# A static instruction order planned for two DMA queues that together get 0.76 of the full rate, with two more chunks of keys transposed on TensorE and half the margin on transposing DMAs

## The chip, the cores and the metric

The kernel runs on one core of a Trainium2 chip. The metric is the device time of one execution in microseconds (us). A run that takes over 1.5% more than the fastest run of the same kernel in the same call (one batch of runs on one chip) is called slow; all others are fast. A ratio is the mean time of one kernel's fast runs over the mean of the other's fast runs of the same rounds, so it is not quite the ratio of the medians quoted. "Span" is the time from the first to the last instruction of the one execution that was profiled, about 2 us less than its device time.

## The reference, cut to what matters

Causal linear attention with a decay per head (4 batches, 8 heads, 768 positions, head size 64), done in blocks with a state that is carried on, and after it a feed-forward layer with SiLU over the 3072 x 512 result.

```python
for b in range(nb):                       # blocks of one sequence
    intra = einsum('bhic,bhjc->bhij', qb, kb) * Dmask
    intra = einsum('bhij,bhjd->bhid', intra, vb)
    inter = einsum('bhid,bhde->bhie', qb * lam_pow, kv_state)
    out[:, :, sl] = intra + inter
    kv_state = lam_block * kv_state + einsum('bhsd,bhse->bhde', kb * rev_pow, vb)
...
x = out as (3072, 512)
h = x @ w_in                              # 512 x 2048
return (h / (1 + exp(-h))) @ w_out        # 2048 x 512
```

## The kernel before

The work is cut into 24 chunks of 128 positions and 12 FFN groups of two chunks. Chunks 0 to 5 (batch 0) use one form of attention. Chunks 6 to 23 use another and are loaded in nine segments of two chunks each: a q load, eight pieces of k, eight pieces of v. The first segment is issued on the SP queue, the other eight on GpSimd's.

Every instruction is first described as an operation with its dependences. A small planner, run at build time, then simulates engines and DMA queues and writes each engine's instructions down in the order in which its simulation started them. On the chip each engine follows that order whether or not the simulation was right: an instruction that waits holds up all that stand behind it on the same engine. These are the planner's parts that the change touches.

```python
LATE = 60000.0      # ns of the plan's own time
LADD = 6000.0
EFF = 0.9
STEP = 12.5
...
        live = [f for f in queue if queue[f]]          # "HW" (SP) and "POOL" (GpSimd)
        for f in live:
            cap = STEP * (0.5 * EFF if len(live) == 2 else 1.0)
            ...                                        # serves the queue's first transfer
                op.seen = t + 700.0 + (1.5 * op.bytes / op.rate if op.rate == 170.0 else 0.0)
...
                    margin = LADD if e == "PE" and t > LATE else 0.0
                    for d in op.deps:
                        s = d.seen + (margin if d.bytes else 0.0)   # d.bytes: d is a DMA
```

`seen` is when the plan believes that a transfer is visible. TensorE reads no load directly; the only DMAs it depends on directly are transposing ones, so the margin concerns these alone. Whether a chunk's keys are transposed on TensorE (with an eviction, a copy out of TensorE's output memory PSUM, by VectorE or ScalarE) or by a DMA is a matter of its number.

```python
    def prep_k(c):
        if c < NPET:                                   # NPET = 10
            ...
                for s in range(2):
                    for p in range(NP):                # NP = 4
                        nc.tensor.transpose(ps.tile[:, s, p, :], cols(s, p), ident)
            ...                                        # eviction on VectorE or ScalarE
        else:
            ...
                nc.sync.dma_start_transpose(out=tk.tile..., in_=kb.tile...)
```

## Time and profile before

| | before |
|---|---|
| device time, median of the first 3 runs | 229.15 us (228.57 to 237.23) |
| span of the profiled run | 228.1 us (device time 230.11 us, mean clock 0.987) |
| TensorE busy | 213.9 us (94%) |
| TensorE waits after the first 30 us | five, 7.1 us together |
| VectorE + ScalarE idle at the head of a cast or scaling of a load, until a DMA landed | 65 us |

No fast run of this kernel was profiled. So wherever its trace is set beside that of a fast run below, a slow run stands beside a fast one, and the difference is likely larger than between fast runs; the ratios are of fast runs alone.

The last row is the sum, in the list of who waited for whom, of the waits of VectorE and ScalarE on DMA at the lines that turn loaded q, k and v into bf16 or scale them (k and v of batch 0, 2.4 us, left out). These are VectorE's two largest (columns: us in total, times, longest):

```profile
DVE vs L574 <- DMA big<-in_v_dram: 17.9, 6, 6.4
DVE kseg L422 <- DMA big<-in_k_dram: 10.9, 5, 5.8
```

The lines that show TensorE's own waits are in the prediction.

### The profile page before, as it was taken

To read this page: it belongs to the slowest core of one execution; us is meant where nothing else is said; L and a number is where in the kernel's file an instruction comes from. 1 tells how busy PE (TensorE), PEld (TensorE's weight loads), DVE (VectorE), ACT (ScalarE), POOL (GpSimd) and SP (SyncE) were. 2 spreads that over 40 slices of the span, in tenths; PEclk is the share of its full clock that TensorE was granted. 3 is DMA by queue.
4 is the path that set the end of the run, shared out by engine and by line. 5 is a ranking of instruction groups with operands and counts; after the bars stand their busy time and mean duration, and the time that the engine had idled before them with its cause. 6 is when DMAs were issued, how large, how long until landed. Compare 5 with 4: busy or idle time off the path is not lost.

```text
span 228.1 us, 5382 instructions
## 1 busy us (share of the span) xinstructions
PE 213.9 (94%) x2177; PEld 150.5 (66%) x2177; DVE 121.0 (53%) x260; ACT 116.5 (51%) x218; POOL 88.9 (39%) x152
## 2 busy tenths in 40 slices
PE   8998999999999999999996987997799999999991
PEld 5686876665975875966853864783584885865840
DVE  3887864766897836557408624832626554202011
ACT  5669797763775682844821641642461361441510
POOL 3000000198979568596953964946300000000000
PEclk9999999999999999999997999999999999999997
DMA  5999999999966999999999999999790301202204
GB/s 140 333 295 388 328 331 333 278 237 223 237 150 129 226 204 170 233 152 231 178 171 155 198 177 138 171 211 137 147 182 19 78 3 33 62 0 46 49 0 92
DMA packets 49400, 39.15 MB, mean 172 GB/s; under 512 B 28896, under 2 KB 39136, under 8 KB 49376
## 3 DMA queue, kind: packets, MB, share of 16 engines
q1 hardware_dynamic: 43984, 26.22, 56.3%
q0 software_dynamic: 5248, 12.59, 26.7%
q8 instruction: 17, 0.28, 0.6%
q14 instruction: 7, 0.06, 0.1%
q10 hardware_dynamic: 144, 0.00, 0.0%
HBM read 27.27 MB, written 6.29 MB: 147 GB/s over the span
## 4 chain that ended last, share of the span: by engine, by line
DMA 37%; PE 29%; POOL 17%; SPq 6%; issue 4%; ACT 3%; DVE 1%; POOLq 0%
DMA big<-in_k_dram 23%; POOL big L406 15%; PE h L820 13%; DMA qf<-in_q_dram 12%; PE o L852 12%; SPq L354 6%; DMA big<-in_v_dram 2%; POOL qf L354 2%; PE op L645 1%; ACT g L828 1%; SPq L447 1%; PE sc L621 1%; PE sc L966 0%; ACT w_out_bf L454 0%; ACT w_in_bf L454 0%
## 5 line engine op out<-in xcount | busy, mean ns | idle before, releaser
L820 PE MATMUL h<-x,w_in_bf 128*128 128x256 bf16 x768 | 91.7, 273 | 0.0
L852 PE MATMUL o<-w_out_bf,g 128*128 128x512 bf16 x384 | 90.9, 382 | 0.0
L820 PEld LDWEIGHTS <-w_in_bf 128*128 128x128 bf16 x768 | 72.8, 98 | 10.7 <-ACT w_in_bf L454 0.2
L828 ACT ACTIVATE g<-h 128x512 bf16<-128x512 f32 x96 | 56.4, 595 | 37.7 <-PE h L820 37.2
L852 PEld LDWEIGHTS <-g 128*128 128x128 bf16 x384 | 35.5, 98 | 35.4 <-issue 0.6
L406 POOL DMA_DIRECT2D big<-in_k_dram x64 | 39.3, 620 | 18.9 <-DMA qf<-in_q_dram 12.7
L406 POOL DMA_DIRECT2D big<-in_v_dram x64 | 39.7, 627 | 11.4 <-DMA big<-in_k_dram 9.5
L866 DVE COPY ob<-o 128x512 f32<-128x512 f32 x17 | 11.7, 687 | 28.0 <-PE o L852 28.0
L679 DVE CAST sbd<-kv 64x256 bf16<-64x256 f32 x38 | 16.0, 422 | 11.7 <-PE kv L665 6.9
L574 DVE TENSOR_TENSOR vs<-big,tab 128x512 bf16<-128x512 f32 x18 | 12.2, 689 | 18.1 <-DMA big<-in_v_dram 17.9
L420 ACT ACTIVATE kseg<-big 64x512 bf16<-64x512 f32 x19 | 11.8, 628 | 16.3 <-DMA big<-in_v_dram 7.6
L627 DVE TENSOR_TENSOR ss<-sc,mask 128x512 bf16<-128x512 f32 x18 | 12.4, 689 | 7.4 <-PE sc L621 7.2
L480 POOL COPY gt__97<-qf 1x1 f32<-1x1 f32 x1 | 0.4, 437 | 39.1 <-DMA qf<-in_v_dram 39.1
L692 DVE TENSOR_TENSOR x<-op,tabo 128x512 bf16<-128x512 f32 x18 | 12.4, 690 | 5.7 <-PE op L645 5.4
L645 PE MATMUL op<-ss,vbd 128*128 128x64 bf16 x144 | 11.6, 195 | 4.0 <-DVE ss L627 4.0
L677 ACT ACTIVATE sbd<-kv 64x256 bf16<-64x256 f32 x28 | 10.5, 375 | 9.2 <-PE kv L665 6.8
L367 ACT ACTIVATE qb<-qf 128x512 bf16<-128x512 f32 x11 | 6.9, 629 | 15.6 <-DMA qf<-in_q_dram 15.6
L422 DVE CAST kseg<-big 64x512 bf16<-64x512 f32 x17 | 7.4, 445 | 14.0 <-DMA big<-in_k_dram 10.9
L966 PE MATMUL sc<-zt 128*128 128x256 bf16 x77 | 13.5, 319 | 1.1 <-DVE zt L266 1.1
L665 PEld LDWEIGHTS <-kseg 128*128 128x128 bf16 x132 | 8.0, 98 | 6.9 <-issue 3.7
L665 PE MATMUL kv<-vs,kseg 128*128 128x64 bf16 x132 | 9.2, 193 | 3.1 <-DVE sbd L679 3.1
L645 PEld LDWEIGHTS <-sbd 128*128 128x128 bf16 x132 | 9.4, 99 | 3.4 <-issue 2.7
(73 smaller groups left out, 178.5 us busy)
## 6 DMA issues: line engine op xcount, KB each, us to landing
out_dram<-ob SPq DMA_DIRECT2D x48, 128.0 KB, 3.7
big<-in_moe_w_in_dram SPq DMA_DIRECT2D x4, 1024.0 KB, 9.6
big<-in_moe_w_out_dram SPq DMA_DIRECT2D x4, 1024.0 KB, 7.6
qf<-in_q_dram POOLq DMA_DIRECT2D x8, 512.0 KB, 6.9
big<-in_k_dram POOLq DMA_DIRECT2D x64, 64.0 KB, 7.0
big<-in_v_dram POOLq DMA_DIRECT2D x64, 64.0 KB, 4.6
qf<-in_q_dram SPq DMA_DIRECT2D x3, 512.0 KB, 10.2
qf<-in_k_dram SPq DMA_DIRECT2D x2, 512.0 KB, 8.9
```

The source lines that it names most:

```text
L354: QS[eng].dma_start(out=tf.tile[:, hh].rearrange("s h t d -> s h (t d)"), in_=r[:, hh])
L406: QS[eng].dma_start(out=t.tile[hs, o:o + n, p, :], in_={"k": k, "v": v}[which][b, hh, 64 * c0:64 * (c0 + n), :].rearrange("(c s) d -> s c ...
L574: nc.vector.tensor_tensor(tv.tile, i, t[:, :, :, None].to_broadcast([128, 2, NP, D]), op=AL.mult)
L627: nc.vector.tensor_tensor(sb.tile.rearrange("a s p b -> a (s p) b"), ps.tile.rearrange("a s p b -> a (s p) b"), mask1[:, None].to_broadcas ...
L645: nc.tensor.matmul(o_cols(p, sub), lhsT=l, rhs=r, start=not ovs["started"], stop=i == len(steps) - 1, skip_group_check=True)
L665: nc.tensor.matmul(kvp.tile[:, p, :], lhsT=kcols(s, p), rhs=tv.tile[:, s, p, :], start=st, stop=True, skip_group_check=True)
L679: nc.vector.tensor_copy(nb.tile[hs, :, h, :], kvp.tile[hs])
L692: nc.vector.tensor_tensor(xt[g].tile[:, :, C * off:C * off + C], ob.tile, tabo[:, :, C * blk:C * blk + C], op=AL.mult)
L820: nc.tensor.matmul(hb.tile[:, i, :], lhsT=w_in_bf[:, ko, m * 128:(m + 1) * 128], rhs=xt[g].tile[:, ko, :], start=(ko == 0), stop=(ko == 3) ...
L828: nc.scalar.activation(gb.tile, hb.tile.rearrange("a i n -> a (i n)"), AF.Silu)
L852: nc.tensor.matmul(po.tile, lhsT=gt.tile[:, g0 + mt * C:g0 + (mt + 1) * C], rhs=w_out_bf[:, m, cs], start=(m == 0), stop=(m == 15))
L966: nc.tensor.matmul(zp, lhsT=zt[:, 0:128], rhs=zt, start=nz == 0, stop=True, skip_group_check=True)
```

## The change

Its intent: let the plan expect slower loads while both queues have work, so that the fixed orders fit what the chip does; take two transposing DMAs off the SP queue; and, as the factor now says more of the truth, halve a cushion that had stood in for it.

```diff
-NPET = 10
-NPETQ = 12
+PETK = tuple(range(6, 12))
+PETQ = tuple(range(0, 12, 2))
...
-LADD = 6000.0
-EFF = 0.9
+LADD = 3000.0
+EFF = 0.76
...
-        if c < NPETQ:
+        if c in PETQ:
...
-        if c < NPET:
+        if c in PETK:
```

The queries' set is unchanged. Keys of chunks 6 to 9 were on TensorE already, so 10 and 11 are new.

## The prediction

> **What bounds the kernel now.** I read the page's busy shares first, then who waited for whom with TensorE as the waiter, then the busy time by stretch, cut at the moments when GpSimd issues the q load of the next segment of two chunks (45.25, 58.09, 70.35, 85.36, 99.47, 112.33, 129.66 and 145.38 us; the last load of all is issued at 162.24), and last the instructions in order of time around each TensorE wait.
>
> ```profile
> PE 213.9 (94%) x2177; PEld 150.5 (66%) x2177; DVE 121.0 (53%) x260; ACT 116.5 (51%) x218; POOL 88.9 (39%) x152
> ```
>
> TensorE is the bound: 213.9 of 228.1 us busy, no other engine over 53%. The chain that ended last names DMA for 37% and POOL for 17%, but it follows one path of releases back through the loads; TensorE beside it was hardly ever empty. So the question is where its missing time lies.
>
> ```profile
> PE op L645 <- DVE ss L627: 4.0, 3, 2.2
> PE kv L665 <- DVE sbd L679: 3.1, 2, 2.0
> ```
>
> (columns: us in total, times, longest). Five waits of 2.17, 1.99, 0.35, 1.16 and 1.46 us, 7.1 us together, ending at 123.18, 138.00, 144.07, 155.59 and 163.62. Everything else is the start-up before 6 us, 0.6 us near 18, and about 5 us after the last matmul at 223.
>
> ```profile
> 58.10:70.40 12.30, 12.30 (x160) 10.00 (x158) 11.04 (x23) 9.22 (x18) 10.74 (x18) 1.00 0.71 179
> 70.40:85.40 15.00, 15.00 (x155) 10.85 (x153) 9.20 (x21) 10.09 (x19) 10.67 (x18) 1.00 1.07 198
> 85.40:99.00 13.60, 13.60 (x156) 10.30 (x154) 8.22 (x18) 8.23 (x18) 10.42 (x17) 1.00 1.17 200
> 99.00:112.30 13.30, 13.30 (x135) 8.95 (x134) 8.59 (x19) 6.02 (x12) 10.85 (x18) 1.00 1.21 209
> 112.30:129.70 17.40, 15.22 (x137) 10.28 (x136) 8.12 (x18) 6.46 (x13) 10.93 (x19) 0.90 1.08 163
> 129.70:145.40 15.70, 13.36 (x117) 8.78 (x116) 7.77 (x16) 6.33 (x12) 10.72 (x18) 1.00 1.11 169
> 145.40:162.50 17.10, 15.60 (x146) 10.76 (x144) 6.92 (x17) 7.08 (x14) 10.38 (x17) 1.00 1.19 158
> ```
>
> (stretch, its length, busy us of PE, PE weight load, DVE, ACT, POOL, then granted clock, DMA share, GB/s). TensorE is full to 112 us. The holes lie in the last three segments, the ones that take longest (17.4, 15.7, 17.1 us against 12.3 to 15.0 before), with the DMA engines at a share over 1 throughout. After 163.6 TensorE is full to the end: 60 us of work is still queued when the last load lands, so the loads as such do not set the end. How can TensorE wait, then?
>
> ```profile
> 117.99 0.40 PE L621 MATMUL sc<-qT,kT 128*128 128x64 bf16 x8
> ...
> 121.98 0.43 DVE L369 CAST qb<-qf 128x512 bf16<-128x512 f32 x1 [0.88 <-DMA qf<-in_q_dram]
> ...
> 122.44 0.69 DVE L627 TENSOR_TENSOR ss<-sc,mask 128x512 bf16<-128x512 f32 x1
> ...
> 123.18 0.21 PE L645 MATMUL op<-ss,vbd 128*128 128x64 bf16 x1 [2.17 <-DVE ss L627]
> ...
> 123.95 1.89 PE L852 MATMUL o<-w_out_bf,g 128*128 128x512 bf16 x4
> ```
>
> The scores were ready at 118.4. VectorE, in the order written at build time, first stood before casts of loads that had not landed (a v load until 119.31, a q load until 121.98), and TensorE, in its own fixed order, stood before the matmul that needs the masked scores although FFN matmuls lay behind it. The other waits have the same form: VectorE before a v load (released 135.76), a q load (154.35) or a k load (161.38). The plan expected these landings earlier than they came.
>
> **What the Trainium skill says.** "TensorE: Matmul & The Clock Gate", Architectural detail: ACT and DVE are strict FIFO; TensorE can only pull weight loads ahead. The lines above agree. Same page, Part 1: after an idle window of about 3.4 us the array clock is halved. Here 2.17 us of idle were enough: the four FFN matmuls after 123.95 took 1.69 us start to start, against 0.86 normally, and the granted clock of that stretch is 0.90; the 1.99 us hole at 138 cost no clock. "DMA: Bandwidth & Descriptors", Queues, rings and completion order: each DMA engine round-robins between the queues with work. That is what the plan's factor models. "Advanced Engine Details and Errata", X-Bar Transpose: transposing DMAs are as fast as plain ones; this trace does not look so:
>
> ```profile
> out_dram<-ob SPq DMA_DIRECT2D x48, 128.0 KB, 3.7
> ...
> kT<-kseg SPq DMA_TRANSPOSE x14, 8.3
> qT<-qb SPq DMA_TRANSPOSE x6, 6.4
> ```
>
> (last column: median us to landing). A transpose of 256 KB takes 6.4 to 8.3 us, a 128 KB store 3.7.
>
> **The change part by part.**
>
> *Factor 0.9 to 0.76.* It acts in the plan only while the SP and the GpSimd queue both hold transfers: each then gets half the factor. The kernel's own rates, used here only to see how the order shifts, give per segment on GpSimd one q of 524288 B at 300 and 16 pieces of 65536 B at 186 B/ns, 7.4 us alone; on SP three transposes of 262144 B at 170 and four stores of 131072 B at 386, 6.0 us alone. SP drains in 6.0/0.45 = 13.3 us, meanwhile GpSimd has done 6.0 of 7.4 and needs 1.4 more: 14.7 us. With 0.76: 6.0/0.38 + 1.4 = 17.2 us. Measured: 12.8, 12.3, 15.0, 14.1, 12.9, then 17.3, 15.7 and about 17. So 0.9 fits the early segments and is too hopeful in just the three where TensorE waits; 0.76 fits those and is too cautious before. The new order should put casts and attention later among the FFN work, and the heads of the queues should no longer be blocked. Before 44.6 us, where GpSimd's first load is released, nothing should move.
>
> *Margin 6000 to 3000 ns.* Added, after 60 us, to the planned landing of a transposing DMA that a TensorE operation reads directly. It halves a cushion; the factor makes up part of it. At present TensorE has no wait on a DMA at all, and the first score matmuls on such keys (85.49 us) come 16 us after the issue at 69.65, so cushion there is.
>
> *Keys of chunks 10 and 11 on TensorE.* Chunks 6 to 9 are there already; the queries keep their set (0, 2, ... 10 is the same six). Added: 16 transposes and two evictions.
>
> ```profile
> 57.05 1.06 PE L547 MATMUL h<-ident,kseg 128*128 128x128 bf16 x16
> 57.94 1.04 PE L820 MATMUL h<-x,w_in_bf 128*128 128x256 bf16 x8
> ```
>
> Sixteen take 57.94 - 57.05 = 0.89 us of TensorE, on the bound: +0.9 us. The evictions of 128x1024 take 0.68 us on VectorE or 1.02 on ScalarE, beside other work at 53 and 51%. Removed: the two transposing DMAs issued at 69.65. The segment without any transpose took 12.3 us, the next, with three, 15.0; estimate: two fewer let the later loads come about 2 us earlier, which is cushion for the five waits and no gain of its own.
>
> **Sum.** Waits to be won: 7.1 us, and I take 70% (5.0), since a static order on a jittery DMA seldom loses all of them. The half-clock phase cost about 1.6 us (0.3 on the 16 attention matmuls, 0.8 on four FFN ones, 0.2 each on the next eight and eight); the profiled run took 230.11 us, 1.5 more than the fastest at 228.57, so I suppose that only some runs have it, and count 0.8. Less 0.9 for the transposes: 5.0 + 0.8 - 0.9 = 4.9 us, 229.15 - 4.9 = 224.3 us. Floor with all waits and the dip gone: 229.15 - 7.1 - 1.6 + 0.9 = 221.3.
>
> **Rivals.** (1) The waits only move: a new order creates other blocked heads, or TensorE now waits on the transposes themselves because of the halved margin. For it: nothing couples the plan to the chip, and holes began as soon as the pace changed. Against: late plans are harmless while FFN work is queued, and 60 us of it is left. Time: 227 to 230. (2) The plan becomes so late that it slows the loads: casts sit later in the fixed order, the three staging buffers come free later, the load stage runs beyond 162 us. This alone costs nothing, as 60 us of work follow and the last group needs only some 14 us of FFN (64 by 0.109 and 32 by 0.216), unless the FFN backlog runs dry; per segment TensorE has 14 us of FFN and about 2 of attention, 16, against the planned 17.2, so the backlog shrinks by about 1 us per segment. It could end in holes of a few us near the end: 226 to 231. (3) All waits vanish: 221 to 222.5. The deep backlog speaks for it.
>
> **Range and chances.** 221.0 to 229.5 holds (3) and most of (1). Two per cent is 4.6 us, just under my 4.9, so faster and same are near even: 0.48 and 0.45. Slower by 2% would need new holes of over 11 us: 0.07.
>
> **What will show it.** Right: the waits of TensorE on L645 and L665 shrink from 7.1 to 1 to 3 us, clock 1.00 in every stretch, busy TensorE time up by about 0.9 us apart from the dip, 48 key transposes on L547 in place of 32, 12 transposing DMAs of keys in place of 14, VectorE's waits for loads moved to where nothing behind them is urgent. Wrong: a TensorE wait released by a DMA (the margin), by casts or stores newly in the way, or idle TensorE after 165 us with the last load later than about 175 (rival 2).

## The result, and the profile after

The changed kernel took 221.34 us (median of four runs, 220.55 to 222.35), beside 230.7 us for the kernel before (four runs, 228.57 to 237.23). The ratio is 0.9658 (95% interval 0.9596 to 0.972): faster by 3.4%. Six runs on another occasion gave 220.65 us and 0.9731 (0.967 to 0.979). The result lies within the predicted range, near its lower end.

The page's busy line for TensorE, after the change:

```profile
PE 212.1 (97%) x2193; PEld 150.1 (68%) x2193; DVE 120.5 (55%) x256; ACT 117.8 (54%) x224; POOL 89.1 (41%) x152
```

The span is 219.3 us, 8.8 less. TensorE's busy time fell by 1.8 us although it now runs 16 more matmuls, and its idle time fell from 228.1 - 213.9 = 14.2 to 219.3 - 212.1 = 7.2 us, so by 7.0. Together that is the 8.8. The 7.0 is, within 0.1 us, the sum of the five waits. This is a slow run against a fast one; by the two ratios fast runs differ by about 8 and 6 us (estimates: 221.4 and 220.6 us over the ratio, less themselves). All waits of TensorE that are left (us in total, times, longest):

```profile
PE sc L966 <- DVE zt L266: 1.1, 1, 1.1
PE h L505 <- DVE kb L364: 0.5, 2, 0.3
PE h L505 <- ACT g L828: 0.4, 1, 0.4
PE h L720 <- DVE qT L513: 0.3, 1, 0.3
```

All four are in the first 19 us. L645 and L665, which had held the five waits, are gone from the list, and no wait ends on a DMA. Busy time of the engines by stretch, cut again at GpSimd's q loads (columns as in the prediction):

```profile
57.26:69.60 12.34, 12.34 (x153) 9.93 (x152) 9.23 (x19) 8.65 (x15) 10.63 (x17) 1.00 0.75 190
69.60:82.30 12.70, 12.56 (x165) 9.88 (x164) 11.79 (x25) 8.84 (x18) 10.76 (x18) 1.00 0.65 177
...
111.00:127.30 16.30, 16.30 (x165) 11.73 (x163) 8.97 (x19) 8.12 (x17) 10.78 (x18) 1.00 1.02 172
127.30:142.85 15.55, 15.55 (x140) 11.00 (x138) 7.61 (x16) 7.91 (x16) 10.88 (x19) 1.00 1.13 196
142.85:156.70 13.85, 13.85 (x139) 9.52 (x138) 7.98 (x16) 5.98 (x12) 10.68 (x17) 1.00 1.03 176
```

Two things are to be seen. The first number after the length equals the length in the last three rows: TensorE is full where it had holes, at clock 1.00, while the DMA engines are about as loaded as before (a share of 1.02 to 1.13) and two of the three late segments still take 15.6 and 16.3 us. So it is not fast loads that filled TensorE; they were no longer waited for. (The load stage, from GpSimd's first load to its last, did get 6.0 us shorter, 117.0 to 111.0; with the factor alone it took 113.1.) And the second row, the segment that lost its two key transposes, takes 12.7 us, where before it took 15.0.

The place that had held the longest wait, now in order of time:

```profile
117.41 0.40 PE L621 MATMUL sc<-qT,kT 128*128 128x64 bf16 x8
117.64 2.75 PE L852 MATMUL o<-w_out_bf,g 128*128 128x512 bf16 x12
117.85 0.69 DVE L627 TENSOR_TENSOR ss<-sc,mask 128x512 bf16<-128x512 f32 x1 [4.77 <-PE sc L621]
```

Before, the masking of these scores (L627) stood behind casts of loads that had not come, and started 4 us after the scores were done (122.44 against 118.39). Now VectorE is the one that is waiting, 4.77 us, for TensorE, and masks at once. This is the whole change in one line: the wait moved from the engine that is the bound to one that is not. In the list of VectorE's waits:

```profile
DVE ss L627 <- PE sc L621: 19.4, 7, 4.8
...
DVE kseg L422 <- DMA big<-in_v_dram: 0.7, 1, 0.7
```

The wait on v loads at L574, 17.9 us before, is gone, and the sum over VectorE and ScalarE of idle time at the heads of loads fell from 65 to 4.7 us.

How wrong was the plan? These are the times at which the plan itself (printed at build time by the kernel's own planner) issues GpSimd's eight q loads and its last piece, and when the chip did:

```
                    q loads of eight segments                               last piece
plan, before     42.4   55.9   69.7   82.8   96.0  109.3  122.2  135.9     147.7
chip, before     45.3   58.1   70.4   85.4   99.5  112.3  129.7  145.4     162.2
chip - plan - 2.9  0    -0.7   -2.2   -0.3    0.6    0.2    4.6    6.7      11.7
plan, after      42.4   58.0   72.9   84.4   99.4  115.7  131.9  149.0     163.9
chip, after      45.0   57.3   69.6   82.3   97.0  111.0  127.3  142.9     156.0
chip - plan - 2.6  0    -3.3   -5.9   -4.7   -5.1   -7.4   -7.3   -8.7     -10.5
```

(2.9 and 2.6 us is by how much the chip starts the first one later.) Before, the chip kept up with the plan as far as the sixth q load and then fell behind, by 11.7 us in the end; the first of TensorE's five waits (123.18) lies in the segment in which it begins to, the others in the two after it. With 0.76 the chip is ahead of the plan at every segment.

### The profile page after: what moved, and what is told of

The parts are those of the page before. It is cut to its first block, busy times and chain, and to the rows that moved or that the text cites. A ratio compares the mean times of both kernels' runs of the same rounds, so it can differ in the third digit from the quotient of the medians.

```text
span 219.3 us, 5399 instructions
## 1 busy us (share of the span) xinstructions
PE 212.1 (97%) x2193; PEld 150.1 (68%) x2193; DVE 120.5 (55%) x256; ACT 117.8 (54%) x224; POOL 89.1 (41%) x152
## 4 chain that ended last, share of the span: by engine, by line
PE 79%; DMA 8%; SPq 6%; ACT 3%; DVE 1%; issue 0%
PE o L852 34%; PE h L820 34%; DMA qf<-in_q_dram 8%; SPq L354 6%; PE op L645 4%; PE sc L621 2%; PE kv L665 2%; ACT g L828 1%; PE h L547 1%; PE h L505 1%; DVE ob L866 1%; PE op L786 1%; SPq L447 1%; PE sc L966 0%; ACT w_out_bf L454 0%
## 5 line engine op out<-in xcount | busy, mean ns | idle before, releaser
L852 PE MATMUL o<-w_out_bf,g 128*128 128x512 bf16 x384 | 89.9, 379 | 0.0
L406 POOL DMA_DIRECT2D big<-in_k_dram x64 | 39.6, 625 | 14.7 <-DMA qf<-in_q_dram 12.8
L677 ACT ACTIVATE sbd<-kv 64x256 bf16<-64x256 f32 x38 | 14.3, 376 | 24.7 <-PE kv L665 18.6
L866 DVE COPY ob<-o 128x512 f32<-128x512 f32 x15 | 10.4, 690 | 29.3 <-PE o L852 28.3
L627 DVE TENSOR_TENSOR ss<-sc,mask 128x512 bf16<-128x512 f32 x18 | 12.4, 687 | 19.5 <-PE sc L621 19.4
L679 DVE CAST sbd<-kv 64x256 bf16<-64x256 f32 x28 | 11.8, 422 | 15.1 <-PE kv L665 9.0
L864 ACT ACTIVATE ob<-o 128x512 f32<-128x512 f32 x9 | 5.4, 597 | 18.0 <-PE o L852 17.9
L422 DVE CAST kseg<-big 64x512 bf16<-64x512 f32 x24 | 11.5, 499 | 1.2 <-DMA big<-in_v_dram 0.7
L574 DVE TENSOR_TENSOR vs<-big,tab 128x512 bf16<-128x512 f32 x18 | 11.9, 683 | 0.1
L585 DVE COPY vbd<-vs 64x512 bf16<-64x512 bf16 x36 | 11.3, 314 | 0.4
L645 PE MATMUL op<-ss,vbd 128*128 128x64 bf16 x144 | 11.4, 193 | 0.0
L645 PE MATMUL op<-qT,sbd 128*128 128x64 bf16 x132 | 10.8, 193 | 0.1
L645 PEld LDWEIGHTS <-vbd 128*128 128x128 bf16 x144 | 9.3, 98 | 1.5 <-issue 0.2
L966 PEld LDWEIGHTS <-zt 128*128 128x128 bf16 x77 | 7.8, 112 | 3.2 <-DVE zt L266 1.1
```

Of the source, the lines that this page charges most:

```text
L406: QS[eng].dma_start(out=t.tile[hs, o:o + n, p, :], in_={"k": k, "v": v}[which][b, hh, 64 * c0:64 * (c0 + n), :].rearrange("(c s) d -> s c ...
L574: nc.vector.tensor_tensor(tv.tile, i, t[:, :, :, None].to_broadcast([128, 2, NP, D]), op=AL.mult)
L627: nc.vector.tensor_tensor(sb.tile.rearrange("a s p b -> a (s p) b"), ps.tile.rearrange("a s p b -> a (s p) b"), mask1[:, None].to_broadcas ...
L645: nc.tensor.matmul(o_cols(p, sub), lhsT=l, rhs=r, start=not ovs["started"], stop=i == len(steps) - 1, skip_group_check=True)
L677: nc.scalar.activation(nb.tile[hs, :, h, :], kvp.tile[hs], AF.Copy)
L852: nc.tensor.matmul(po.tile, lhsT=gt.tile[:, g0 + mt * C:g0 + (mt + 1) * C], rhs=w_out_bf[:, m, cs], start=(m == 0), stop=(m == 15))
```

## The experiments

Three theories were to be told apart. **Lateness**: TensorE waits only where the plan expects loads earlier than they come, so it is the factor that does it. **Relief**: two transposing DMAs fewer let the loads come in time. **Luck**: any other order would scatter as much. A summary first; the last two columns are of the profiled run, and the waits leave out idle that the profile puts down to "issue" (0.3 us or less, 0.5 in e10).

| run | factor | margin, ns | keys on TensorE | median us (lowest to highest, runs) | ratio to before (95%) | TensorE waits after 30 us | VectorE + ScalarE idle at heads of loads |
|---|---|---|---|---|---|---|---|
| before | 0.9 | 6000 | 6-9 | see text | 1 | 7.1 (slow run) | 65 |
| the change | 0.76 | 3000 | 6-11 | 221.34 (220.55-222.35, 4) | 0.966 (0.960-0.972) | 0 | 4.7 |
| e1_eff_only | 0.76 | 6000 | 6-9 | 224.12 (223.68-224.96, 4) | 0.985 (0.979-0.992) | 2.9 | 6.3 |
| e2_keys_only | 0.9 | 6000 | 6-11 | 234.22 (231.16-241.23, 4) | 1.019 (1.009-1.029) | 7.4 | 41 |
| e3_margin_only | 0.9 | 3000 | 6-9 | 235.29 (234.29-236.42, 4) | 1.034 (1.027-1.042) | 10.8 | 58 |
| e6_no_keys | 0.76 | 3000 | 6-9 | 224.01 (222.38-224.13, 4) | 0.983 (0.976-0.989) | 2.3 | 5.3 |
| e4_no_margin | 0.76 | 6000 | 6-11 | 222.63 (221.37-223.72, 4) | 0.987 (0.976-0.998) | 0.7 | 8.8 |
| e5_no_eff | 0.9 | 3000 | 6-11 | 231.01 (228.58-232.1, 4) | 1.021 (1.009-1.034) | 5.8 | 36 |
| e7_cushion | 0.9 + cushion | 6000 | 6-9 | 221.72 (219.87-226.91, 4) | 0.981 (0.970-0.992) | 3.9 (slow run) | 30 |
| e8_eff_083 | 0.83 | 3000 | 6-11 | 228.67 (223.81-229.67, 4) | none, one fast run | 1.9 | 36 |
| e9_eff_070 | 0.70 | 3000 | 6-11 | 224.76 (224.45-226.3, 4) | 0.993 (0.983-1.002) | 2.9 | 2.9 |
| e10_late_cushion | 0.9 + late cushion | 6000 | 6-9 | 227.06 (222.3-230.21, 6) | none, one fast run | 6.4 (slow run) | 34 |
| e11_change_again | 0.76 | 3000 | 6-11 | 220.65 (220.15-221.08, 6) | 0.973 (0.967-0.979) | 0 | 3.6 |
| e12_no_margin_again | 0.76 | 6000 | 6-11 | 222.23 (221.1-223.02, 6) | 0.980 (0.973-0.987) | 1.1 | 6.1 |

e1, e2, e3 and e6 ran in one call, then e4, e5, e7 and e8, then e9 to e12. The kernel before had medians of 228.29, 227.14 and 230.29 us in these calls (8, 8 and 11 runs), from 223.76 to 245.65, with 3, 4 and 8 slow runs. The three calls ran on three chips. The record's verdict is "faster" for the change's own call and "unclear" for every later run that has a ratio, so those ratios are to be read with their intervals. All kernels gave the right result.

Luck is all but out: the 28 runs with factor 0.76 (four kernels, six rows) took 220.15 to 224.96 us, the 12 runs of the three changed kernels with 0.9 and no cushion 228.58 to 241.23, and the kernel before 223.76 and more.

### The changed kernel again

No edit; it stood beside the last three runs.

> The changed kernel itself, unaltered, so that it stands on the same chip beside the next three. All theories: 220.5 to 222.5 us, no TensorE wait after 30 us over 0.3 us, runs within 2 us of each other and clock at 0.994 or more in each.

Measured: 220.65 us, six runs within 1 us, no TensorE wait over 0.2 us after 30 us. All as expected.

### The factor alone

```diff
-LADD = 3000.0
+LADD = 6000.0
-PETK = tuple(range(6, 12))
+PETK = tuple(range(6, 10))
```

(against the changed kernel). Expected:

> The factor 0.76 alone; margin 6000 ns and keys 6 to 9 as in the kernel before. Pace theory (TensorE waits only where the plan expects loads earlier than they come; the factor makes it late enough): the five waits of TensorE on VectorE, 7.1 us, fall under 1.5 us, no half-clock phase, TensorE does not pay the 0.9 us of 16 transposes: 220 to 222.5 us. Relief theory (the two transposing DMAs fewer are what lets the loads come in time): waits stay at 4 us or more, 226 us or more. Luck theory (any other order would do as well or as badly): anything from 221 to 231.

Measured: 224.12 us. The half-clock phase and the five old waits are gone, as the lateness theory wants, and idle at the heads of loads fell to 6.3 us. But 2.9 us of new waits are there, which it had not foreseen, so the time is 1.6 us above its range. None of them follows a late load; the run without the new keys tells what they are.

### The other two parts alone

The keys alone, against the changed kernel:

```diff
-LADD = 3000.0
-EFF = 0.76
+LADD = 6000.0
+EFF = 0.9
```

The margin alone:

```diff
-PETK = tuple(range(6, 12))
-EFF = 0.76
+PETK = tuple(range(6, 10))
+EFF = 0.9
```

> Keys of chunks 10 and 11 on TensorE alone; factor 0.9, margin 6000 ns. Pace theory: the plan still issues its last load about 12 us too early (and 2 us earlier still, as it too has two transposes fewer), so TensorE waits 5 to 9 us: 227 to 232 us. Relief theory: waits under 2 us, 222 to 224 us. Luck theory: anything from 221 to 231.

> Margin 3000 ns alone; factor 0.9, keys 6 to 9. Pace theory: waits as before or more, some of them now released by a transposing DMA: 228 to 233 us. Relief theory: as before, 228 to 231 us. Luck theory: anything from 221 to 231.

Measured: 234.22 and 235.29 us, both slower than the kernel before. Relief is thereby out: with two transposing DMAs fewer and nothing else, TensorE waited 7.4 us. In that run and in the one with the margin alone, the longest waits are:

```profile
128.64 0.21 PE L645 MATMUL op<-ss,vbd 128*128 128x64 bf16 x1 [3.84 <-DVE ss L627]
```

```profile
163.81 0.37 PE L645 MATMUL op<-ss,vbd 128*128 128x64 bf16 x4 [4.24 <-DVE ss L627]
```

The form is the old one: TensorE before a masking that VectorE had not got to. In the margin run no wait is released by a DMA; the expectation that transposes themselves would be waited for was wrong. The margin alone took 2 us more than was expected (233 us at most). The median of the keys alone holds two slow runs; its two fast ones, 231.16 and 232.64 us, lie at the upper end of what was expected (232).

### Without the new keys

```diff
-PETK = tuple(range(6, 12))
+PETK = tuple(range(6, 10))
```

> Factor 0.76 and margin 3000 ns without the keys of chunks 10 and 11. Pace theory: no waits, and 0.9 us less TensorE work than the changed kernel: 220 to 222 us, same or slightly below it. Relief theory: loads come too late by the 2 us or so of the two DMAs, waits of 4 us or more: 226 us or more. If the backlog of FFN work runs dry late, idle TensorE after 160 us of 1 to 4 us: 222 to 225 us.

Measured: 224.01 us, in the band that was foreseen for a backlog that runs dry late, and not the 220 to 222 of plain lateness. TensorE has 0.9 us less to do than in the changed kernel and is still slower. At the first of its waits (this kernel, then the changed one, at the same place):

```profile
74.57 0.28 PE L665 MATMUL kv<-vs,kseg 128*128 128x64 bf16 x4
...
75.78 0.28 PE L665 MATMUL kv<-vs,kseg 128*128 128x64 bf16 x4 [0.69 <-ACT sbd L677]
```

```profile
74.12 0.28 PE L665 MATMUL kv<-vs,kseg 128*128 128x64 bf16 x4
74.47 1.06 PE L547 MATMUL h<-ident,kseg 128*128 128x128 bf16 x16
...
75.36 0.28 PE L665 MATMUL kv<-vs,kseg 128*128 128x64 bf16 x4
```

From one update of the state to the next, TensorE needs the copy of the state in between (L677). Here no FFN matmul was left to fill that time. In the changed kernel the 16 new transposes stand in exactly this gap, and the next update comes 1.24 us after the last one, against 1.21 without them: they cost nothing there. The keys are also ready sooner: the scores of chunk 10 start at 76.89 us, against 86.22 without, and chunk 10's FFN work is there to fill later gaps. The other waits of this run, 0.67 at 170.69 and 0.80 at 187.53, are of the same kind:

```profile
187.53 1.03 PE L820 MATMUL h<-x,w_in_bf 128*128 128x256 bf16 x8 [0.80 <-DVE x L692]
```

An FFN matmul waits for the attention result that it is to read. That nothing else was ready is read from the plan, so it is what the plan believed and not what the chip had: the plan starts any operation that it believes ready, and it has TensorE idle for 1.8 us at 72, 1.0 at 152, 1.8 at 169 and 2.0 at 186.6 of its own time.

### Without the new margin, twice

```diff
-LADD = 3000.0
+LADD = 6000.0
```

> The whole change except that the margin stays at 6000 ns. Backlog theory (with factor 0.76 the loads are no longer waited for; what is left in the two runs without the new keys, 2 to 3 us, are moments when the FFN backlog is dry because attention is placed too late, and the plan itself shows these holes, at 72, 168 and 188 us of its own time): this plan has holes of its own of 0.9, 1.6 and 1.0 us at 73, 168 to 170 and 185, so TensorE idles 1 to 2.5 us there: 222 to 223.5 us. Margin does not matter: 221 to 221.6 us, no wait after 30 us.

> The change with the margin of 6000 ns again, now beside the changed kernel. If the margin of 3000 is worth something by itself (attention placed earlier, so the FFN backlog is not dry near 170): 0.5 to 1.5 us slower than the changed kernel, with a TensorE wait near 170 us. If the 1.3 us between the two earlier were the chip: within 0.4 us of it.

Measured: 222.63 us in one call and 222.23 in the next, where the changed kernel stood beside it with 220.65. Each of the six runs without the margin took longer than each of the six with it (221.1 to 223.02 against 220.15 to 221.08), so the margin seems worth up to 1.6 us. But the two intervals of the ratios (0.973-0.987 and 0.967-0.979) overlap, and only 0.44 us of it is seen as a wait, at 171 us. Of the 2.6 us between the spans of the two profiled runs (221.1 and 218.5), 1.6 were there when GpSimd issued its first load (45.88 and 44.28 us), where both kernels have the same instructions in the same order (the plans first differ at 97 us). So the start-up alone can differ by 1.6 us between two profiled runs, which bears on every small difference here. How much the margin gives is left open; that it gives something is likely.

### Without the factor

```diff
-EFF = 0.76
+EFF = 0.9
```

> The whole change except that the factor stays at 0.9. Pace theory: the two other parts make the plan more hopeful still (margin alone 235, keys alone 234), so 232 to 240 us with 7 us or more of waits on VectorE or ScalarE heads and clock under 0.99. Relief theory is gone already; if the keys do need the margin to work, 222 to 226 us.

Measured: 231.01 us, with 5.8 us of waits, 36 us of idle at the heads of loads and clock 0.992 in the profiled run, 0.985 to 0.991 in the others. It is a little better than expected and slower than before by its interval. Without the factor the other two parts are a loss in every combination that was run.

### Lateness got in another way

The kernel before, with a cushion on loads in the plan (60000 ns on; in the second form from 85000 ns on):

```diff
+LCAST = 8000.0     # second form also: LATEC = 85000.0, in place of the new LATE below
-  margin = LADD if e == "PE" and t > LATE else 0.0
+  margin = LADD if e == "PE" and t > LATE else LCAST if e in ("DVE", "ACT") and t > LATE else 0.0
```

> Kernel before with factor 0.9, margin 6000 ns and keys 6 to 9, and a cushion of 8000 ns added in the plan to every load that a VectorE or ScalarE operation reads after 60 us. Lateness theory (it is enough that the casts are placed later than the loads come, however that is got): waits fall from 7 to under 3 us: 222 to 226 us. If only the slower pace itself helps, because lateness grows from segment to segment: waits of 5 us or more remain at the late segments, 227 us or more.

> Kernel before (factor 0.9, margin 6000 ns, keys 6 to 9) with the 8000 ns cushion on loads, but only after 85 us of the plan's time, where the measured loads begin to fall behind it. The plan has no hole and TensorE has 0.9 us less to do than in the changed kernel. Lateness theory: no wait over 1 us, 219.5 to 222 us, level with the changed kernel or up to 1 us below it. If the cushion of the other run owed its fast runs to luck, or needs its early part: 224 us or more.

The first took 219.87, 221.03 and 222.41 us in its three fast runs and 226.91 in a slow one. Nothing of the change is in this kernel, and its fast runs are level with the changed kernel's (by the ratio, 0.981 against 0.966 and 0.973, not quite): so it is likely the placing of the casts that counts, and not the factor as such. Its profiled run is the slow one; that the waits are gone in its fast runs is not shown. The second missed its expectation: 227.06 us, one fast run of six (222.3). In both profiled runs, slow ones, the loads are still waited for, 30 and 34 us in all. In that of the second the last segment still comes later than 8 us of cushion allow:

```profile
169.07 0.69 DVE L576 TENSOR_TENSOR vs<-big,tab 128x512 bf16<-128x512 f32 x1 [7.96 <-DMA big<-in_v_dram]
...
170.41 0.21 PE L647 MATMUL op<-qT,sbd 128*128 128x64 bf16 x1 [3.83 <-DVE x L694]
```

(the lines are two lower in this kernel.) VectorE stood 8 us before a v load, and TensorE 3.83 us before what lay behind it. A cushion of fixed size is used up by a lag that grows from segment to segment; a factor on the rate grows with it. This is argued from one slow run; no run tests it. That the early part of the cushion was needed as well, as the second form leaves it out, can't be excluded.

### More and less of the factor

```diff
-EFF = 0.76
+EFF = 0.83      # in the other run: 0.70
```

> The whole change with a factor of 0.83 in place of 0.76. The plan's last load is issued at 151.3 us of its own time, about 154 on the chip's clock, 2 to 3 us before it could come. Lateness theory: a wait or two in the last segments, 1 to 4 us in all, 222 to 226 us, between the changed kernel and the run with 0.9. Luck theory: no order between the factors, over 228 possible.

> The whole change with a factor of 0.70: too late on purpose. Backlog theory: the plan has holes of its own, 3 us between 71 and 76, 1.6 at 170 to 172 and 2.0 at 187.5; the chip, ahead of the plan, shows part of them, 1.5 to 5 us of TensorE waits released by VectorE or ScalarE, none of which follows a late load: 222.5 to 226 us. If later is only ever better: 221 to 221.6 us.

With 0.83 the four runs took 223.81, 228.99, 228.36 and 229.67 us. The profiled one is the fast one; it has only 1.9 us of waits after 30 us, but 36 us of idle at the heads of loads, in the range of the runs with 0.9. The size was expected at 222 to 226, so this is worse than foreseen, and no profile shows where the slow runs lost it. With 0.70 the chip never waits for a load in earnest (2.9 us), the runs are within 2 us of each other, and the time is 224.76 us: TensorE waits 2.9 us, nearly all on attention results and copies, among them

```profile
188.45 1.03 PE L820 MATMUL h<-x,w_in_bf 128*128 128x256 bf16 x8 [0.80 <-DVE x L692]
```

So later is not only ever better. Of the four factors tried with the full change (0.9, 0.83, 0.76 and 0.70), 0.76 is the best, and both sides show their own kind of wait.

## Why the prediction was right or wrong

**Right: what bounds the kernel and what the factor does.** The prediction read the five waits as heads of fixed queues blocked by loads that came later than planned, and the factor as the cure. The factor alone took idle at the heads of loads from 65 to 6.3 us; every run with 0.76 or 0.70 has under 9 us of it, every run with a higher factor 30 or more.

Its hand count of the pace was right in direction and too long in size: it gave 14.7 us a segment for 0.9, while the plan's own q loads are 12.9 to 13.8 us apart (mean 13.4, as on the chip up to the sixth). The chip kept step as far as the sixth q load and lost 11.7 us after it. One of the five readings was also off: the wait that ended at 155.59 is put down to a q load at 154.35, but VectorE was at work without a gap from 151.80, when it had stood 3.91 us before a v load. The form is the same.

Of the signs, the waits at L645 and L665 went, the clock is 1.00 in the stretches shown, and there are 48 key transposes and 12 transposing DMAs of keys. TensorE's busy time apart from the half-clock phase did not rise by 0.9 us: it fell by 1.8, of which the phase explains 1.6.

**Mis-sized: "I take 70% (5.0), since a static order on a jittery DMA seldom loses all of them".** All 7.1 us went; TensorE's idle time fell by 7.0. The chip ran up to 10.5 us ahead of the new plan, which is more slack than any jitter seen here took back. The prediction's own floor of 221.3 us, its third rival, is what came: 221.34. That they agree to 0.1 us is luck: the floor takes the waits of a slow run (230.11 us) off a median of 229.15, and it holds the 0.9 us below.

**Mis-sized: "count 0.8" for the half-clock phase.** In the profiled run the whole 1.6 us went. The supposition that only some runs have it fits the later calls: its fast runs there took 223.8 to 228.5 us at mean clocks of 0.987 to 1.00, its slow ones 227.5 to 245.7 at 0.964 to 0.995. All ten runs of the changed kernel have 0.994 or more, and they lie between 220.15 and 222.35 us.

**Probably wrong in sign: "Sixteen take ... 0.89 us of TensorE, on the bound: +0.9 us".** The 0.89 us is right as a duration, but the transposes fill a gap that TensorE has anyway once the plan is late. With the keys on TensorE the time is 2.7 to 3.4 us lower than without (221.34 or 220.65 against 224.01), but these are different calls (220.65 and 224.01 on different chips). The traces account for 1.4 of it: 2.3 us of waits less, 0.9 of work more; another 1.2 are start-up waits before the two orders differ. By the ratios the gain is 0.983 against 0.966 and 0.973 with the margin at 3000, and not clear at 6000 (0.985 without the keys, 0.987 and 0.980 with them). "No gain of its own", said of the relief of the queue, was right: the segment did get about 2 us shorter (15.0 to 12.7), but keys alone were slower than before. The prediction treated the parts as a sum. They are not one.

**The rivals.** New blocked heads (1) are what the two smaller parts give without the factor. A backlog that runs dry (2) is real and was dismissed too lightly: it costs the factor alone 2.9 us; with the keys 0.4 us is left of it after 60 us, with keys and margin nothing. Its other half, loads slowed beyond 162 us, did not happen: the last piece was issued at 156.0 us.

**A step that was not sound.** The prediction took 6.4 to 8.3 us for a transpose of 256 KB against 3.7 for a store of 128 KB as a sign that transposing DMAs are slower than plain ones. By the byte the two are about equal, and the time to landing depends on what else is in the queues (a 64 KB piece of k took 7.0 us), so nothing here speaks against the page that was cited.

## What to carry to other kernels

Where engines follow a fixed order, idle time of an engine that is not the bound is not free: look at what stands behind the instruction that waits, and let slack lie on the side of expecting transfers too late. Calibrate the planner with the measured pace of the stage in which waits occur, rather as a rate than as a fixed cushion (which did as well here in three of four runs, but its profiled run still lost 30 us at such heads), and stop where the work that fills the bound engine's gaps begins to run dry. Try the parts of such a change together as well as alone: here two of three were losses by themselves, and beside the third they were probably gains.

## What the Trainium skill lacked or had wrong

- "TensorE: Matmul & The Clock Gate", Part 1: the clock is said to halve after an idle window of about 3.4 us. Here a hole of 2.17 us was followed by about 3 us at half clock (granted clock 0.50 from 123.18 to 126.20 us; four FFN matmuls in 1.69 us instead of 0.86), and one of 1.99 us was not. Over all profiled runs, slow ones too, seven TensorE waits of 2.17, 2.20, 2.29, 2.73, 3.83, 3.84 and 4.24 us were followed by it (granted clock 0.50 to 0.57 in the next 3 us); one of 2.92 us was not, and none of those of 1 to 2 us after the start-up set it off. The page says that the window runs freely; of a single hole shorter than the window it says nothing.
- "DMA: Bandwidth & Descriptors", Queues, rings and completion order: it tells that the queues with work take turns, and gives no rate for plain loads beside transposes and stores. Here the core moved 327 GB/s with the weights and first loads alone (30 to 40 us of the kernel before) and 158 to 169 GB/s in the three late segments, at a DMA share of 1.08 to 1.19. The late k and v loads also come in 64 KB pieces, those early loads in 512 KB and 1 MB, so the fall is not shown to come from the mix alone.
- No page that was read says how the strict order of ScalarE and VectorE turns a late load into a wait of TensorE. The runs give it a size: 65 us of idle at such heads beside 7.1 us of TensorE waits, 4.7 us beside none.
